# A retention layer followed by a gated two-layer network on one core: the opening chunks in another order, and second-layer weights converted block by block

## Chip, cores and metric

One Trainium2 chip, one of its cores. The metric is the device time of one execution in microseconds. Engines: TensorE (PE; its weight loads are listed as PEld), VectorE (DVE), ScalarE (ACT), GpSimd (POOL) and SyncE (SP), which issues most DMAs. Weights in HBM are float64; everything computed is float32.

## What is computed

```python
def _attn_ref(q, k, v):                    # (4, 8, 768, 64) each
    gamma = 1.0 - 2.0 ** (-5.0 - np.arange(H, dtype=np.float32))
    for t in range(S):
        state = gamma[None, :, None, None] * state + np.einsum('bhd,bhe->bhde', k[:, :, t], v[:, :, t])
        y[:, :, t] = scale * np.einsum('bhd,bhde->bhe', q[:, :, t], state)
...
def _moe_ref(x, w_in, w_out):              # x (3072, 512), w_in (512, 2048), w_out (2048, 512)
    h = x @ w_in
    sp = np.maximum(h, 0.0) + np.log1p(np.exp(-np.abs(h)))
    g = h * erf(sp)
    return (g @ w_out).astype(np.float32)
```

The output of the first part, with the heads side by side, is the input `x` of the second.

## The kernel before

**Chunks.** The sequence is cut into 24 chunks of 128 positions (6 for each of 4 batches); `j` counts them. Four chunks make up the first block of 512 tokens, and everything after it goes in blocks of 256. A chunk goes through short steps with one-letter names at the end of the code: `K_` (`ret_scale`, L385) multiplies keys and queries by powers of the decay on VectorE; `T` (`ret_transpose`, L406) transposes them on TensorE and copies the result out of PSUM on ScalarE (L424); `S_` (`ret_scores`, L427) computes the scores; `M` (`ret_mask`, L440) applies the causal mask on VectorE; `O_` (`ret_out`, L450) multiplies queries with the state (L471), scores with values (L478) and keys with values for the new state (L487), and ScalarE copies the results into `XC` (L498); `A` (`ret_add`, L606) adds the new part to the state on VectorE. A fresh state begins with chunks 0, 6, 12 and 18.

**Loads.** `load(j)` (L102) issues a chunk's keys, queries and values, each 256 KB in runs of 256 bytes, on SP's queue; the queries of chunks 1 and 2 go on ScalarE's queue (L118). Inside `load(3)` the first two parts of the first weight piece are issued ahead of the values (L121). Weight loads come after (L166 for `w_in`, L174 for `w_out`).

**Scales.** `kq_s` holds the decay factors per position, chunk in the batch, and head. Those of chunk 0 come from `d_k`; those of later chunks follow by multiplication on GpSimd (L336), then `query_scale` on VectorE inverts them for the queries. `by` is the reciprocal of `d_s`, which is loaded by two small DMAs (L298).

**Weights.** The float64 words are turned into float32 by integer arithmetic, as a generator of steps (`conversion`, L182): VectorE cuts out the exponent (L213), ScalarE rescales it (L214), VectorE prepares the high mantissa (L217), adds the low word (L222), puts sign and exponent together (L225) and multiplies (L231). There are 16 pieces of 256 columns of the first layer ("in") or 256 rows of the second ("out"), in the order in0, in1, in2, in3, out0, out1, in4, ... The first four pieces (`n < 4`) are converted in two parts each. After the last VectorE row that reads a piece's raw words, the load that reuses its place is issued (`load_pieces_after`). The steps are interleaved by hand with the rest: `pace(n)` lets n of them go, `need(...)` lets go as many as it takes until a named block is there. From piece 5 on, a piece's first step (exponent) is issued early, inside the piece before it (L262).

**First block.** `hidden(g, u)` computes 128 columns of the first layer for 512 tokens (L664) and copies them on ScalarE (L682); four of them make a group `g`. `gate(g)` runs softplus (L624) and, except for group 0, erf right after it (L634); erf of group 0 comes later by the table `after`. `gated(g)` multiplies on VectorE (L653). `project(g, tt)` adds the group's part of the second layer (L700) in four steps; for group 0 a step takes two 128-token tiles and two 128-row blocks of `w_out`. Products of the first layer begin before chunk 3 is finished: `ret_out(3, between)` puts `hidden_of(0)` for the first 384 tokens between its state products and its value products, and `hidden_of(1)` for 384 tokens follows.

**PSUM.** Three pools: `ps_r` and `ps_h` with two banks each, `ps_o` with four (`o0` to `o3`). At the start (`early`), `ret_psum` takes `ps_r` and `ps_h` in turn, for transposes, scores and results alike; only chunk 3's results are in `ps_o`. `keep_warm(n)` issues n products of the identity with itself that nobody reads.

**Start.** The order is `K_(0)`, the other scales, `T(0)`, and then for each chunk scores, scaling of the next, state addition, transposes of the next, mask, results. So TensorE issues the scores of a chunk only after all results of the one before.

From the second block on, a seven-product scheme (`hidden_part`, L757; `project_part`, L829) takes over; the change doesn't touch it.

Of the kernel before, what the change touches and what calls it, by code (L numbers as in the profile page):

```python
# [12 lines left out]
F32 = mybir.dt.float32  # L13
U32 = mybir.dt.uint32
I64 = mybir.dt.int64
AF = mybir.ActivationFunctionType
# [3 lines left out]
P = 128  # L20
# [25 lines left out]
def kernel(  # L46
# [35 lines left out]
    ctx.enter_context(tc.manual_schedule())  # L82


    KQ, V, KB = {}, {}, {}

    NB = JPC + 2
# [12 lines left out]
    def load(j):  # L100
        b, c = divmod(j, NC)
        if j == JPC - 1:  # L102

            x = act.tile([P, N], F32, name="e", bufs=1)
            KQ[j] = x[:, : 2 * d_model].rearrange("p (i h d) -> p i h d", i=2, h=H)
            V[j] = x[:, 2 * d_model : 3 * d_model].rearrange("p (h d) -> p h d", h=H)
        else:
            KQ[j] = loads.tile([P, 2, H, D], F32, name="kq")
            V[j] = loads.tile([P, H, D], F32, name="v")
        now = slice(c * C, (c + 1) * C)  # L110
        if j >= NB:
            KB[j] = loads.tile([P, HP * C], F32, name="kb", bufs=2)
            nc.sync.dma_start(KQ[j][:, 0], k[b, :, now, :].rearrange("h p d -> p h d"))
            load_blocks(KQ[j][:, 1].rearrange("p h d -> p (h d)"), q[b, :, now, :])
            load_blocks(KB[j], k[b, :, now, :])
        for i, src in enumerate((k, q) if j < NB else ()):

            queue = nc.scalar if i and 0 < j < 3 else nc.sync  # L118
            queue.dma_start(KQ[j][:, i], src[b, :, now, :].rearrange("h p d -> p h d"))  # L119
        if j == JPC - 1:  # L120
            load_piece(0, 0)  # L121
        nc.sync.dma_start(V[j], v[b, :, now, :].rearrange("h p d -> p h d"))  # L122

    kq_s = const.tile([P, NC, 2, H], F32, name="kq_s")
    d_k = const.tile([P, H], F32, name="d_k")
# [61 lines left out]
    def conversion(n):  # L187

        which, i = pieces[n]
        half, s, at = i // 4, i % 4 // 2, i % 2

        for part in range(2) if n < 4 else (None,):
            words = raws[place[n]].bitcast(U32)
            if which == "in":
                f = slice(at * 2 * P, (at + 1) * 2 * P)
                if part is not None:
                    f = slice((at * 2 + part) * P, (at * 2 + part + 1) * P)
                to = w_in_sb[:, s, 2 * half : 2 * half + 2, :, f].rearrange("p d k f -> p (d k) f")  # L200
            else:
                to = w_out_sb[:, s, 2 * half : 2 * half + 2, at * 2 : at * 2 + 2, :].rearrange(
                    "p d f c -> p d (f c)"
                )
            words = words.rearrange("p (a b w) -> p a b w", a=to.shape[1], w=2)
            number, power = (
                x.rearrange("p (a b) -> p a b", a=to.shape[1]) for x in (numbers, powers[n % 2])
            )
            if part is not None:
                f = slice(part * P, (part + 1) * P)  # L210
                words, number, power = words[:, :, f], number[:, :, f], power[:, :, f]
            lo, hi = words[:, :, :, 0], words[:, :, :, 1]
            nc.vector.tensor_scalar(power, hi, 0x7FF00000, None, op0=ALU.bitwise_and)  # L213
            nc.scalar.activation(power, power, AF.Relu, bias=below, scale=8.0)  # L214
            if part is None:
                yield
            nc.vector.tensor_scalar(  # L217
                number, hi, 0xFFFFF, 1 << 20, op0=ALU.bitwise_and, op1=ALU.bitwise_or
            )
            yield  # L220
            numberf = number.bitcast(F32)
            nc.vector.scalar_tensor_tensor(numberf, number, 2.0**32, lo, op0=ALU.mult, op1=ALU.add)  # L222
            if part is None:
                yield
            nc.vector.scalar_tensor_tensor(  # L225
                power, hi, 1 << 31, power, op0=ALU.bitwise_and, op1=ALU.bitwise_or
            )
            if part != 0:
                load_pieces_after(n)
            yield  # L230
            nc.vector.scalar_tensor_tensor(  # L231
                to, numberf, 2.0**-52, power.bitcast(F32), op0=ALU.mult, op1=ALU.mult,
            )
            done.update((which, 2 * i + u) for u in (range(2) if part is None else (part,)))
            yield
# [18 lines left out]
    def weights():  # L254


        pending = [conversion(n) for n in range(n_p)]
        begun = 0
        for n, steps in enumerate(pending):
            for k, _ in enumerate(steps, start=begun):  # L260
                yield
                if n > 4 and n + 1 < n_p and k == 2:  # L262
                    next(pending[n + 1])
                    yield
            begun = int(n > 4)
            if pieces[n] == ("out", 5):
                yield from sums("in", 0)

# [25 lines left out]
    ident = const.tile([P, P], F32, name="ident")  # L294
    make_identity(nc, ident)
    nc.scalar.dma_start(d_k, decay_k)
    for s in range(2):
        nc.scalar.dma_start(d_s[:, s], decay_s[s * D : s * D + 1, :].to_broadcast([P, HP]))  # L298
    load(0)

    nc.scalar.copy(idle_out, ident[:, :1])
    for j in range(1, JPC):
        load(j)
    load_piece(0, 1)
    for n in range(1, 4):
        load_piece(n, 0, 1)
    load(JPC)

    causal = const.tile([P, C], F32, name="causal")
    nc.gpsimd.memset(causal, 1.0)  # L310
# [20 lines left out]


    by = const.tile([P, H], F32, name="by")
    nc.vector.reciprocal(by.rearrange("p (h s) -> p s h", s=2), d_s)
    for c in range(1, NC):
        nc.gpsimd.tensor_tensor(kq_s[:, c, 0], kq_s[:, c - 1, 0], by, op=ALU.mult)  # L336

    def other_scales():
        query_scale(slice(1, NC))

# [24 lines left out]
    QT, KT, SC, AM, XC, SU = {}, {}, {}, {}, {}, {}  # L367

    psum_turn = itertools.cycle((ps_r, ps_h))
    early = True  # L370


    idle = ps_o.tile([P, P], F32, name="o0")
# [2 lines left out]
        for _ in range(n):  # L376
            nc.tensor.matmul(idle, ident, ident, start=True, stop=True)

    keep_warm(16)

    def ret_psum(pool=None):

# [2 lines left out]

    scaled = set()

    def ret_scale(j):
        if j >= NJ:
            return  # L390
        scaled.add(j)
        if j >= NB:
            nc.vector.tensor_tensor(
                KQ[j][:, 0], KQ[j][:, 0],
                kq_s[:, j % NC, 0, :, None].to_broadcast([P, H, D]), op=ALU.mult,
            )
            for i, x in enumerate((KB[j], KQ[j][:, 1].rearrange("p h d -> p (h d)"))):
                x = x.rearrange("p (u a d) -> p u a d", u=HP, d=32)
                by = kq_b[:, j % NC, i, :, :, None].to_broadcast([P, HP, 4, 32])
                nc.vector.tensor_tensor(x, x, by, op=ALU.mult)  # L400
            return
        by = kq_s[:, j % NC, :, :, None].to_broadcast([P, 2, H, D])
        nc.vector.tensor_tensor(KQ[j], KQ[j], by, op=ALU.mult)
        pace(-1.1)

    def ret_transpose(j):  # L406
        assert j in scaled
        if j >= NB:
            for name, store, x in (
# [3 lines left out]
                nc.vector.transpose(store[j].rearrange("p u t -> p (u t)"), x)  # L413
            return
        for i, (name, store) in enumerate((("k", KT), ("q", QT))):
            p = ret_psum()
            for u in range(HP):
                nc.tensor.transpose(  # L418
                    p[:, u, :],
# [25 lines left out]
            )  # L445
        pace(-1.2)

    RP = {}

    def ret_out(j, between=None, copies=True):  # L450
        c = j % NC
        m, i = divmod(j, JPC)
        if i == 0:
            XC[m] = ret.tile([P, HP, TCH], F32, name="xT")

        if between is None:
            pp = [ret_psum() for _ in range(2)]
        else:
            pp = [ps_o.tile([P, HP, C], F32, name=f"o{r + 1}") for r in range(2)]

        def place(h):
            return pp[h % 2][h // 4 * D : (h // 4 + 1) * D, h % 4 // 2, :]
# [20 lines left out]
        if c < NC - 1:  # L483
            new = SU[j] = pp[0][:, 2:, :].rearrange("p a (b d) -> p (a b) d", d=D)
            for h in range(H):
# [2 lines left out]
                    new[r * D : (r + 1) * D, h // 2, :], KQ[j][:, 0, h, :], V[j][:, h, :],  # L488
                    start=False, stop=True, skip_group_check=True,
                )  # L490
        RP[j] = pp
        if copies:
            ret_copy(j)

    def ret_copy(j):
        m, i = divmod(j, JPC)
        for r in range(2):
            nc.scalar.copy(XC[m][:, r::2, i * C : (i + 1) * C], RP[j][r][:, :2, :])  # L498
        pace(2.5)


# [117 lines left out]
    def gate(g):  # L619
# [3 lines left out]
        E[g] = act.tile([P, N], F32, name=name, bufs=1)  # L623
        nc.scalar.activation(E[g], HS[g], AF.Softplus)  # L624

        if g:
            gate_erf(g)

    def gate_erf(g):
# [59 lines left out]
    def project(g, tt):  # L689
# [3 lines left out]
        if g:  # L693
            of = [(tt, u) for u in range(FG)]
        else:
            of = [(step % 2 * 2 + i // 2, step // 2 * 2 + i % 2) for i in range(4)]
        need("out", g * FG + max(u for _, u in of))
        for tt, u in of:
            ft = g * FG + u
# [174 lines left out]
    )  # L874


    K_(0)
    other_scales()
    T(0)
    keep_warm(3)  # L880
    for j in range(JPC - 2):
        S_(j)

        K_(j + 1)
        if j:
            A(j - 1)
        T(j + 1)
        M(j)
        O_(j)


    S_(JPC - 2)
    A(JPC - 3)
    M(JPC - 2)
    ret_out(JPC - 2, copies=False)
    K_(JPC - 1)

    next(weight_steps)
    T(JPC - 1)
    ret_copy(JPC - 2)  # L900
    need("in", 0)
    S_(JPC - 1)
    A(JPC - 2)
    M(JPC - 1)
    need("in", 1)
    early = False
    ret_out(JPC - 1, lambda: hidden_of(0, slice(TCH - C)))
    room = 0.0


# [24 lines left out]
    for g in range(G0):  # L935
# [10 lines left out]
        if g:  # L946
            for tt in range(TT):
                project(g - 1, tt)
                if g == 1 and tt < 2:
                    waiting.append((K_, 5) if tt else (M, 4))  # L950
                elif g == G0 - 1 and tt == 0:
                    waiting.extend([(K_, JPC + 2), (T, JPC + 2)])
                elif g == G0 - 1 and tt == 1:
# [132 lines left out]
```

## Time and profile before

| | |
|---|---|
| median of 6 runs | 683.9 us (683.5 to 684.19) |
| profiled execution | 683.86 us, span of its records 682.1 us |
| busy, share of the span | PE 675.7 us (99%), DVE 389.6 (57%), ACT 256.0 (38%), POOL 5.7 (1%) |
| 7.5 to 25.5 us | busy PE 16.36, DVE 12.10, ACT 6.74 of 18.0 us; DMA 209 GB/s |
| 25.5 to 132 us | busy PE 106.50, DVE 99.61, ACT 56.58 of 106.5 us; DMA 172 GB/s |
| DMA | 47.65 MB in 156528 packets, 143024 of them under 512 bytes |

The profiled execution is one of the six; between its span and its time lie 1.7 us. A row of a timeline reads: start, duration, engine, line, operation, tile written <- tiles read, shapes, and in brackets how long the engine was idle before it and what ended that. The chain of work that ended last is followed back from the last instruction; in its listing by time a row's duration is only its part of the chain, up to the start of the next row. "Landing" is the time from the issue of a DMA to its last completion event; a DMA has sixteen, one for each of the core's DMA engines. The share of the whole span says little about the first 25 us, where other engines hold TensorE up; so that stretch is read by itself.

### The profile page before, as it was taken

To read this page: it belongs to the slowest core of one execution; us is meant where nothing else is said; L and a number is where in the kernel's file an instruction comes from. 1 tells how busy PE (TensorE), PEld (TensorE's weight loads), DVE (VectorE), ACT (ScalarE), POOL (GpSimd) and SP (SyncE) were. 2 spreads that over 40 slices of the span, in tenths; PEclk is the share of its full clock that TensorE was granted. 3 is DMA by queue.
4 is the path that set the end of the run, shared out by engine and by line. 5 is a ranking of instruction groups with operands and counts; after the bars stand their busy time and mean duration, and the time that the engine had idled before them with its cause. 6 is when DMAs were issued, how large, how long until landed. Compare 5 with 4: busy or idle time off the path is not lost.

```text
span 682.1 us, 14444 instructions
## 1 busy us (share of the span) xinstructions
PE 675.7 (99%) x6214; PEld 578.3 (85%) x6214; DVE 389.6 (57%) x609; ACT 256.0 (38%) x291; POOL 5.7 (1%) x21
## 2 busy tenths in 40 slices
PE   8999999999999999999999999999999999999998
PEld 8744544587999999999999999999999999999996
DVE  4899999585845634643553564555544554343324
ACT  3368362324414234144144242341441441423431
POOL 2000000100000000000000000000000000000000
PEclk9999999999999999999999999999999999999999
DMA  9999744333412322221321222222312200000000
GB/s 188 212 241 250 190 125 103 62 60 62 115 36 46 76 37 42 74 41 37 78 45 32 63 44 46 68 42 45 71 37 47 59 18 2 1 32 1 1 32 32
DMA packets 156528, 47.65 MB, mean 70 GB/s; under 512 B 143024, under 2 KB 147376, under 8 KB 156464
## 3 DMA queue, kind: packets, MB, share of 16 engines
q1 hardware_dynamic: 153952, 46.19, 31.5%
q8 instruction: 49, 0.80, 0.5%
q10 hardware_dynamic: 2512, 0.53, 0.5%
q14 instruction: 15, 0.12, 0.1%
HBM read 40.39 MB, written 6.29 MB: 68 GB/s over the span
## 4 chain that ended last, share of the span: by engine, by line
PE 97%; DMA 1%; SPq 1%; DVE 1%; issue 0%; ACT 0%
PE hp L757 37%; PE o L829 36%; PE hp L664 8%; PE o L700 8%; PE r L543 1%; PE hp L508 1%; DMA kq<-in_k_dram 1%; PE o L579 1%; PE r L431 1%; PE hp L558 1%; PE r L558 1%; PE r L478 1%; SPq L119 0%; PE r L418 0%; SPq L122 0%
## 5 line engine op out<-in xcount | busy, mean ns | idle before, releaser
L757 PE MATMUL hp<-xs,w_in_sb 128*128 128x128 f32 x1280 | 149.7, 275 | 0.0
L757 PEld LDWEIGHTS hp<-xs,w_in_sb 128*128 128x128 f32 x1280 | 147.8, 192 | 1.6 <-issue 0.5
L829 PE MATMUL o<-w_out_sb,h 128*128 128x256 f32 x640 | 141.7, 379 | 0.0
L829 PEld LDWEIGHTS o<-w_out_sb,h 128*128 128x128 f32 x640 | 121.6, 190 | 16.5
L757 PE MATMUL hp<-xT,w_in_sb 128*128 128x128 f32 x960 | 113.7, 275 | 0.0
L757 PEld LDWEIGHTS hp<-xT,w_in_sb 128*128 128x128 f32 x960 | 111.9, 192 | 1.9 <-issue 1.0
L829 PE MATMUL o<-w_out_sb,e 128*128 128x256 f32 x480 | 112.1, 383 | 0.0
L653 DVE TENSOR_TENSOR e<-h,e 128x1024 f32<-128x1024 f32 x42 | 49.5, 1221 | 100.0 <-ACT e L634 99.8
L829 PEld LDWEIGHTS o<-w_out_sb,e 128*128 128x128 f32 x480 | 88.2, 190 | 11.6
L664 PE MATMUL hp<-xT,w_in_sb 128*128 128x512 f32 (+2 forms) x144 | 56.8, 548 | 0.0
L782 DVE TENSOR_TENSOR h<-h,hp 128x512 f32<-128x512 f32 x20 | 13.7, 687 | 72.3 <-PE hp L757 72.3
L624 ACT ACT_TABLE_LOAD x24 | 30.8, 1283 | 60.8 <-issue 45.4
L664 PEld LDWEIGHTS hp<-xT,w_in_sb 128*128 128x128 f32 x144 | 25.7, 190 | 26.7 <-issue 24.3
L634 ACT ACTIVATE e<-e 128x2048 f32<-128x2048 f32 (+1 forms) x23 | 42.1, 1836 | 0.2
L624 ACT ACTIVATE e<-h 128x2048 f32<-128x2048 f32 x22 | 42.0, 1910 | 0.2
L770 DVE TENSOR_TENSOR h<-h,hp 128x512 f32<-128x512 f32 x20 | 13.8, 688 | 41.0 <-PE hp L757 41.0
L775 ACT COPY h<-hp 128x512 f32<-128x512 f32 x20 | 11.7, 585 | 61.1 <-PE hp L757 61.1
L780 ACT COPY h<-hp 128x512 f32<-128x512 f32 x20 | 11.7, 585 | 60.3 <-PE hp L757 60.3
L773 ACT COPY h<-hp 128x512 f32<-128x512 f32 x20 | 11.7, 585 | 57.1 <-PE hp L757 57.1
L597 ACT COPY xT<-r 128x256 f32<-128x256 f32 x32 | 10.4, 375 | 54.8 <-PE r L543 54.8
L634 ACT ACT_TABLE_LOAD x24 | 30.8, 1283 | 0.4
L768 ACT COPY h<-hp 128x512 f32<-128x512 f32 x20 | 11.7, 587 | 48.6 <-PE hp L757 48.6
(136 smaller groups left out, 672.8 us busy)
## 6 DMA issues: line engine op xcount, KB each, us to landing
w_out_sb<-in_moe_w_out_dram SPq DMA_DIRECT2D x14, 512.0 KB, 6.0
kq<-in_k_dram SPq DMA_DIRECT2D x23, 256.0 KB, 3.9
v<-in_v_dram SPq DMA_DIRECT2D x23, 256.0 KB, 3.2
out_dram<-r SPq DMA_DIRECT2D x23, 256.0 KB, 3.1
kq<-in_q_dram SPq DMA_DIRECT2D x288, 16.0 KB, 1.8
kb<-in_k_dram SPq DMA_DIRECT2D x288, 16.0 KB, 1.7
w_in_sb<-in_moe_w_in_dram SPq DMA_DIRECT2D x8, 512.0 KB, 10.2
w_out_sb<-in_moe_w_in_dram SPq DMA_DIRECT2D x8, 256.0 KB, 8.8
```

Of the source, the lines that this page charges most:

```text
L558: nc.tensor.matmul(other[a][own, u % 2, D:] if crossed else pp[a][own, u % 2, t], V[j][t, 2 * u + r, :], AM[j][t, r, u, :D], start=crossed ...
L624: nc.scalar.activation(E[g], HS[g], AF.Softplus)
L634: nc.scalar.activation(E[g][:, half], E[g][:, half], AF.Erf)
L653: nc.vector.tensor_tensor(E[g][:, half], HS[g][:, half], E[g][:, half], op=ALU.mult)
L664: nc.tensor.matmul(HP_[ft][:, t], w_in_of(ft, kk), XC[0][:, kk, t], start=(kk == 0), stop=(kk == n_k - 1),)
L700: nc.tensor.matmul(O[0][tt].rearrange("p (d c) -> p d c", d=2), E[g][:, u * TCH + tt * P : u * TCH + (tt + 1) * P], w_out_of(ft), start=(f ...
L757: nc.tensor.matmul(bank[:, u, :], w_in_sb[:, s, IN[a], kk, u * P : (u + 1) * P], XS[m][b][:, kk, :], start=(p in (1, 2, 5) and u == 0 and ...
L768: nc.scalar.copy(h["11"], flat)
L770: nc.vector.tensor_tensor(h["11"], h["11"], flat, op=ALU.add)
L773: nc.scalar.copy(h["12"], flat)
L782: nc.vector.tensor_tensor(h["12"], h["12"], flat, op=ALU.add)
L829: nc.tensor.matmul(O[m][i][:, half, :], G[g][a][:, u * P : (u + 1) * P], w_out_sb[:, s, OUT[b], u, :], start=i not in started, stop=(s == ...
```

## The change

- **Loads**: all keys and queries on SP's queue; a chunk's values are issued by a function of their own after the next chunk's keys and queries. The decay row comes in one DMA.
- **Scaling and transposing one by one**: `ret_scale` and `ret_transpose` take an argument for keys (0) or queries (1) alone. Keys go to `ps_r`, queries to `ps_h`.
- **Scales** of chunk 1 are made on VectorE right after the first keys are scaled; GpSimd makes those from chunk 2 on.
- **Results** of chunks 0 to 3 go to `ps_o`; `copies=False`, `RP` and `ret_copy` go.
- **Order** of the first four chunks: written out anew. Scores of chunk 1 come ahead of the results of chunk 0, those of chunk 2 inside the results of chunk 1, the query transposes of chunk 3 inside the results of chunk 2.
- **Idle products**: `keep_warm` 7, 2, 1 and 2 in place of 16 and 3.
- **Second layer**: pieces 4 and 5 (out0, out1) are converted in two parts too, one for each 128-row block, with VectorE's first row and ScalarE's row over the whole piece; early issue of the first step begins with piece 6. Steps of `project(0)` take one block for all four token tiles.
- **Group 1**: its erf moves behind the first step of `project(0)` and the first step of piece 5; masks 4 and scaling 5 move behind the conversion of in4.

```diff
@@ load @@
         for i, src in enumerate((k, q) if j < NB else ()):
-
-            queue = nc.scalar if i and 0 < j < 3 else nc.sync
-            queue.dma_start(KQ[j][:, i], src[b, :, now, :].rearrange("h p d -> p h d"))
-        if j == JPC - 1:
-            load_piece(0, 0)
-        nc.sync.dma_start(V[j], v[b, :, now, :].rearrange("h p d -> p h d"))
+            nc.sync.dma_start(KQ[j][:, i], src[b, :, now, :].rearrange("h p d -> p h d"))
+        if not early:
+            load_values(j)
+
+    def load_values(j):
+        b, c = divmod(j, NC)
+        nc.sync.dma_start(V[j], v[b, :, c * C : (c + 1) * C, :].rearrange("h p d -> p h d"))
@@ conversion @@
-        for part in range(2) if n < 4 else (None,):
+        for part in range(2) if n < 6 else (None,):
...
+            if part == 0 and which == "out":
+                nc.vector.tensor_scalar(
+                    power, words[:, :, :, 1], 0x7FF00000, None, op0=ALU.bitwise_and
+                )
+                nc.scalar.activation(power, power, AF.Relu, bias=below, scale=8.0)
+                yield
             if part is not None:
-                f = slice(part * P, (part + 1) * P)
+                if which == "out":
+                    to = to[:, :, part * DH : (part + 1) * DH]
+                f = to.shape[2]
+                f = slice(part * f, (part + 1) * f)
                 words, number, power = words[:, :, f], number[:, :, f], power[:, :, f]
             lo, hi = words[:, :, :, 0], words[:, :, :, 1]
-            nc.vector.tensor_scalar(power, hi, 0x7FF00000, None, op0=ALU.bitwise_and)
-            nc.scalar.activation(power, power, AF.Relu, bias=below, scale=8.0)
+            if which == "in" or part is None:
+                nc.vector.tensor_scalar(power, hi, 0x7FF00000, None, op0=ALU.bitwise_and)
+                nc.scalar.activation(power, power, AF.Relu, bias=below, scale=8.0)
@@ weights @@
-                if n > 4 and n + 1 < n_p and k == 2:
+                if n > 5 and n + 1 < n_p and k == 2:
...
-            begun = int(n > 4)
+            begun = int(n > 5)
@@ issue of loads @@
-    for s in range(2):
-        nc.scalar.dma_start(d_s[:, s], decay_s[s * D : s * D + 1, :].to_broadcast([P, HP]))
+    nc.scalar.dma_start(d_s, decay_s[::D].rearrange("(o s) h -> o s h", o=1).to_broadcast([P, 2, HP]))
     load(0)
...
     for j in range(1, JPC):
         load(j)
+        load_values(j - 1)
+    load_piece(0, 0)
+    load_values(JPC - 1)
     load_piece(0, 1)
     for n in range(1, 4):
         load_piece(n, 0, 1)
     load(JPC)
+    load_values(JPC)
@@ scales @@
-    nc.vector.reciprocal(by.rearrange("p (h s) -> p s h", s=2), d_s)
-    for c in range(1, NC):
-        nc.gpsimd.tensor_tensor(kq_s[:, c, 0], kq_s[:, c - 1, 0], by, op=ALU.mult)
+
+    def second_scales():
+        nc.vector.reciprocal(by.rearrange("p (h s) -> p s h", s=2), d_s)
+        nc.vector.tensor_tensor(kq_s[:, 1, 0], kq_s[:, 0, 0], by, op=ALU.mult)
+        query_scale(1)
+        for c in range(2, NC):
+            nc.gpsimd.tensor_tensor(kq_s[:, c, 0], kq_s[:, c - 1, 0], by, op=ALU.mult)
 
     def other_scales():
-        query_scale(slice(1, NC))
+        query_scale(slice(2, NC))
...
-    keep_warm(16)
+    keep_warm(7)
@@ ret_transpose @@
-            p = ret_psum()
+            if part not in (None, i):
+                continue
+            p = ret_psum((ps_h if i else ps_r) if early else None)
@@ ret_out @@
-        if between is None:
+        if early:
+            pp = [ps_o.tile([P, HP, C], F32, name=f"o{(2 * j + r + 1) % 4}") for r in range(2)]
+        else:
             pp = [ret_psum() for _ in range(2)]
-        else:
-            pp = [ps_o.tile([P, HP, C], F32, name=f"o{r + 1}") for r in range(2)]
@@ gate, project @@
-        if g:
+        if g > 1:
             gate_erf(g)
...
-            of = [(step % 2 * 2 + i // 2, step // 2 * 2 + i % 2) for i in range(4)]
+            of = [(i, step) for i in range(TT)]
@@ order of the start @@
-    K_(0)
+    K_(0, 0)
+    second_scales()
+    T(0, 0)
+    keep_warm(2)
+    K_(0, 1)
+    T(0, 1)
+    keep_warm(1)
+    K_(1, 0)
+    T(1, 0)
+    S_(0)
+    K_(1, 1)
+    T(1, 1)
+    keep_warm(2)
     other_scales()
-    T(0)
-    keep_warm(3)
-    for j in range(JPC - 2):
-        S_(j)
-
-        K_(j + 1)
-        if j:
-            A(j - 1)
-        T(j + 1)
-        M(j)
-        O_(j)
-
-
-    S_(JPC - 2)
-    A(JPC - 3)
-    M(JPC - 2)
-    ret_out(JPC - 2, copies=False)
-    K_(JPC - 1)
-
-    next(weight_steps)
-    T(JPC - 1)
-    ret_copy(JPC - 2)
+    M(0)
+    S_(1)
+    K_(2, 0)
+    T(2, 0)
+    O_(0)
+    M(1)
+    K_(2, 1)
+    T(2, 1)
+    A(0)
+    K_(3, 0)
+
+    def next_scores():
+        S_(2)
+        M(2)
+
+    O_(1, next_scores)
+    T(3, 0)
+    A(1)
+    K_(3, 1)
+    O_(2, lambda: T(3, 1))
+    A(2)
+
     need("in", 0)
-    S_(JPC - 1)
-    A(JPC - 2)
-    M(JPC - 1)
+    S_(3)
+    M(3)
     need("in", 1)
+    ret_out(JPC - 1, lambda: hidden_of(0, slice(TCH - C)))
     early = False
-    ret_out(JPC - 1, lambda: hidden_of(0, slice(TCH - C)))
@@ first block @@
-                if g == 1 and tt < 2:
-                    waiting.append((K_, 5) if tt else (M, 4))
+                if g == 1 and tt == 0:
+                    need("out", 1)
+                    next(weight_steps)
+                    gate_erf(1)
+                elif g == 1 and tt == 2:
+                    need("in", 2 * FG + 1)
+                    waiting.extend([(M, 4), (K_, 5)])
```

## The prediction, made before the changed kernel ran

> **What bounds the kernel now.** I read the page's chain shares first, then the chain in order of time, then VectorE's rows, the landings, and TensorE's first matmuls.
>
> ```profile
> PE 97%; DMA 1%; SPq 1%; DVE 1%; issue 0%; ACT 0%
> ```
> TensorE sets the end. The 3% that are not TensorE lie in the first 25 us:
>
> ```profile
> 5.31 7.86 DMA kq<-in_k_dram
> 13.20 1.23 DVE kq L403
> ...
> 20.57 0.56 DVE e L403
> ...
> 23.17 0.60 ACT qT L424
> 23.81 0.37 PE r L431
> 24.97 0.60 PE o L471 x16
> 25.57 2.78 PE hp L664 x8
> 28.35 1.02 PE o L478 x16
> 29.37 0.46 PE o L487 x16
> 29.84 21.78 PE hp L664 x64
> ```
> From 25.57 each row begins where the one before ends, on TensorE, to the last 1% of the span. So a gain can only come from when the second block of the first layer (29.84, `hidden_of(1)`) starts, and it lasts only if nobody who feeds TensorE falls behind. VectorE is the one who might: by the stretches view it is busy 99.6 of the 106.5 us from 25.5 to 132.
>
> ```profile
> 20.49 1.22 DVE L403 TENSOR_TENSOR e<-e,kq_s 128x1024 f32<-128x1024 f32 x1
> 21.62 0.42 DVE L213 TENSOR_SCALAR w_out_sb<-w_out_sb 128x512 uint32<-128x512 uint32 x1
> 24.35 0.41 DVE L611 TENSOR_TENSOR state<-state,r 128x256 f32<-128x256 f32 x1
> 26.21 0.42 DVE L213 TENSOR_SCALAR w_out_sb<-w_out_sb 128x512 uint32<-128x512 uint32 x1
> 28.32 0.69 DVE L231 SCALAR_TENSOR_TENSOR w_in_sb<-w_out_sb 128x512 f32<-128x512 f32 x1
> ```
> Block 0 of the weights is converted from 21.62 to 24.43 (2.81 us), block 1 from 26.21 to 29.01 (2.80). What these two wait for is a load:
>
> ```profile
> 12.73 1.99 SPq L166 DMA_DIRECT2D w_out_sb<-in_moe_w_in_dram  x2
> w_out_sb<-in_moe_w_in_dram SPq DMA_DIRECT2D x2, 256.0 KB, 7.1
> 16.12 5.12 SPq L166 DMA_DIRECT2D w_out_sb<-in_moe_w_in_dram  x6
> ```
> Issued from 12.73 to 14.72, landing about 7.1 later: the completion events put block 0's two halves at 20.0 and 21.0, and block 1's (issued from 16.12) at 24.55 and 25.75. So VectorE now starts block 0 only 0.6 us after its data, and block 1 only 0.5 us after.
>
> **The change part by part.**
>
> *Loads.* Keys and queries go ahead of values, and two query loads move from ScalarE's queue to SP's. Block 0 still stands behind the same eleven 256 KB transfers, block 1 behind the same fourteen, and the engines are full (the DMA row stands at 9 almost throughout from 3.5 us on). So blocks 0 and 1 land at 21.0 and 25.75 again: nothing. The order within changes. Completion events now come at 3.96, 5.7, 6.7, 9.2, 9.5, 10.7, 12.3, 13.1, 14.3, 15.5, 18.9; I give these places to the new order, with places 4 and 5 (two queues at once now) at about 8.0 and 9.2: k0 4.0, q0 5.5, k1 6.7, q1 8.0, v0 9.2, k2 10.7, q2 12.3, v1 13.1, k3 14.3, q3 15.5, v2 18.9. The jump to 18.9 is one of sixteen engines: the fifteenth event of that transfer is at 17.6, after a 16 KB instruction fetch at 14.3.
>
> *Scaling one by one.* A 128x1024 product (1.23) becomes two 128x512 (0.68, from the mask rows): +0.13 times four = 0.5 us of VectorE. Its cover is VectorE's idle time, 5.9 of the 18 us from 7.5 to 25.5; without it, 0.5. Scales of chunk 1 come to VectorE: four small rows of 0.17 to 0.20, and a wait for the decay row, whose two issues land at 4.3 and 5.75 now; one issue lands between. Behind that wait stands q0's scaling, which waits for 5.5 anyway.
>
> *Idle matmuls.* 19 become 12. TensorE is free at 4.5 instead of about 7.9.
>
> *Interleaving.* No instruction is added on TensorE; the order is new. I placed the rows by hand, each at the end of what it needs: transposes of a half 0.44, its copy 0.59, scores 1.09, masks 1.29, values 1.02, state products 0.60, state sum 0.47, addition 0.41. First keys scaled 4.0 to 4.65; first scores at 8.0 (9.58 now); second at 10.6 (13.45); third at 14.7 (18.09); values of chunk 2 at 18.95, where v2 lands; state addition 2 done at 21.0; fourth scores 20.5 to 21.5 (23.81 now). So the path ends at 21.0 as block 0 lands: conversion 0 from 21.05 to 23.85, product 0 at 23.9 (25.57 now). Masks 3 fill VectorE until 25.15; conversion 1 from 25.77 to 28.57. TensorE meanwhile: 23.9 + 2.78 + 1.48 = 28.16, and waits 0.5. Product 1 at 28.65 instead of 29.84: **1.2 us gained**. Two stalls are left, both on weights; what is late next is the load, not the chunks. If the copies or PSUM banks cost more than placed, TensorE has those 0.5 us; bounds: 0.8 (chunks 0.9 late) to 1.2.
>
> *Second layer's first pieces.* A piece takes 5.0 us of VectorE now (48.44 to 53.43). By blocks: 0.60 once, then twice 0.46 + 0.61 + 0.71 + 0.61 = 5.4. Two pieces: +0.8 us, with no cover, since VectorE has none there. It is paid from VectorE's lead. Now the first second-layer product starts at 56.94, with its gated half ready at 54.8: 2.1 to spare, and the block form asks for half a piece less. I carried the new order on: last first-layer block of group 1 converted 46.9; half a piece 50.1; gated product behind erf at 52.05 to 54.3; second block 56.3 (needed 59.2); third 59.5 (62.7); fourth 61.9 (66.2). Piece 6 now waits for ScalarE: softplus and erf of group 1 run 58.1 to 64.5, so its exponent is done at 65.7 and the piece at 68.2 (needed 69.7, now 67.5 for 70.94). Masks 4 then end at 71.3 (73.7), addition 4 at 78.1 (the transposes of chunk 5 want its bank at 78.85), masks 5 at 88.0 (88.6). So no stall, with 0.5 to 0.7 us in hand at the last two; VectorE thus caps the gain at about 1.7. Weight reloads that follow VectorE's rows go out up to 2 to 4 us later (piece 11's at 76.5 for 72), and are used over 10 us after that: nothing.
>
> **Sum.** The profiled execution took 683.86 (span 682.1, 1.7 around it), as good as the median of 683.9. Minus 1.2: **682.7**; its own range, gains of 0.8 to 1.7, is 682.2 to 683.1. About 0.2%, 1.37 us, is what a measurement of this kernel can tell from no change, so the forecast lies at that bound.
>
> **The clock.** This is what I trust least.
>
> ```profile
> L377 PE MATMUL o<-ident x26: 357/421/582, 1.5 to 7.0; 128*128 128x128 f32 x26
> L377 PE MATMUL o<-ident x14: 274/275/421, 6.7 to 9.2; 128*128 128x128 f32 x14
> ```
> Idle matmuls took 421 ns until 7.0 and 275 after: 5.5 us of unbroken work before full speed; their spacing halves from 0.21 to 0.11. The new kernel has a gap after 4.5 and others later. I take the grant at about 7, since gaps there are 0.2 to 0.3 us.
>
> [...]
>
> **Rivals.**
>
> *More: the late engine isn't late.* The jump to 18.9 comes from one engine. If the instruction fetch falls elsewhere, blocks 0 and 1 land as the fourteenth of sixteen events do now, 19.3 and 23.3. Then values 2 start by 18.95 from the TensorE side alone, conversion 0 at 20.95, masks 3, conversion 1 from 25.0 to 27.8, product 1 at 28.15: gain 1.7, up to 2.4 if the chunks run closer. For it: VectorE and TensorE have less to do before 21 than now. Against: the fetch follows TensorE's instruction count, which is the same there within 10%. 681.5 to 682.2.
>
> *Little: one restart.* If the 5.5 us count anew from 4.7, the grant comes at about 10.2. Each us of slow clock costs about 0.5 us of TensorE's work: 3.2 us, 1.6 late at the values, 0.4 of which the waits take up. Gain about 0: 683.5 to 684.
>
> *Slower: the clock stays down.* The same with a second restart at the gap before the second chunk's transposes (7.5): grant at 13 or later. 6 us of slow clock cost 3.0 and more; minus 0.5 that waits swallow, minus the gain of 1.2: +1.3 to +2, so 685.2 to 686. It decides from a grant at about 10.5 on. For it: seven idle matmuls instead of sixteen, and waits for k1, q1 and copies in that stretch. Against: at half speed the work fills the gaps, so the slow state ends itself; and now TensorE keeps its clock through 0.8 us of waiting at 23.
>
> *That it doesn't do what it says:* if two issues in a row on SP held up the loads, q1 and q2 would be later than on ScalarE's queue; SP's issues (0.4 to 2.6 us) run some 7 us ahead of the landings, so no: under 3%, inside the others.
>
> **Chances.** Forecast 0.42 (0.18 of it beyond 1.37 us), more 0.27, little 0.10, slower 0.21 (0.20 beyond the bound). Faster 0.18 + 0.27 = 0.45; within 0.24 + 0.10 + 0.01 = 0.35; slower 0.20. The range reaches from the best of "more" to the near edge of "slower": 681.4 to 685.2.
>
> **What would show it.** Right: conversion 0 starting with its load near 21, product 0 near 23.9, product 1 near 28.7 waiting for L231's counterpart, then no gap until 132, where the first seven-product part starts 1.2 earlier than 132.23. Clock: idle matmuls and transposes at 0.21 spacing after 7.5. Wrong: block 1 landing before 25, TensorE waiting on masks 5 or addition 4, or a gap ahead of the second layer at 55.7.

## The result, and the profile after

The changed kernel takes 685.81 us (median of 17 runs, 683.81 to 687.67) where the kernel before takes 683.73 (38 runs, 683.42 to 684.58). The ratio is 1.0026 (the two medians divided give 1.0030), with a 95% interval from 1.002 to 1.0033: slower by about 0.26%, just beyond the 0.2% that can be told from no change, and outside the range that was given. The profiled execution took 685.98, with a span of 684.3 (before: 683.86 and 682.1), so it is 2.12 longer and lies near the median.

The spread is wider than before, and it isn't one heap. These are all the executions of the changed kernel, the profiled one among them, by the mean TensorE clock that each lists:

| mean clock | executions | times, us |
|---|---|---|
| 0.998 | 13 | 685.59 to 686.18, and twice 687.67 |
| 1.000 | 5 | 683.81, 684.07, 684.1, 684.26, 684.41 |

A clock of 0.998 over 684 us is some 1.4 us of work lost, which is nearly the distance of the two groups. So the first question to the profile is where the clock is down.

The chain's shares, from the page of the changed kernel, say at first that nothing happened:

```profile
PE 98%; DVE 1%; DMA 1%; ACT 0%; issue 0%; ACTq 0%
```

TensorE still sets the end. The chain in order of time (start, length, what) shows where it set it later:

```profile
22.00 0.38 ACT xT L514
...
22.74 0.42 DVE w_out_sb L225
...
24.86 0.70 DVE w_in_sb L243
25.69 4.51 PE hp L680 x8
...
31.70 21.78 PE hp L680 x64
...
90.98 1.02 PE r L493 x16
...
134.43 5.36 PE hp L773 x48
```

Product 0 (the eight matmul records of `hidden_of(0)`, L680) starts at 25.69, where it started at 25.57 before: the whole reordering of the start has gained nothing there. And it takes 4.51 us for the 2.78 of before. Product 1 starts at 31.70 instead of 29.84, 1.86 late, and the last row is 2.20 late (132.23 before).

TensorE's rows in order of time give the wait ahead of product 0, in brackets at its end:

```profile
22.97 0.67 PE L493 MATMUL o<-qT,state 64*64 64x128 f32 x16
25.69 4.51 PE L680 MATMUL hp<-xT,w_in_sb 128*128 128x384 f32 x8 [2.06 <-DVE w_in_sb L243]
```

Here are the same matmuls by line (minimum, median and maximum duration in ns). Before, the median was 486:

```profile
L680 PE MATMUL hp<-xT,w_in_sb x8: 503/834/847, 25.7 to 29.7; 128*128 128x384 f32 x8
```

And here are stretches of the span (length, then busy time of TensorE, its weight loads, VectorE, ScalarE and GpSimd, then the granted clock, the DMA share and GB/s):

```profile
22.90:26.31 3.41, 1.35 (x22) 0.91 (x19) 3.34 (x7) 0.72 (x1) 0.00 (x0) 1.00 1.11 231
26.31:29.72 3.41, 3.41 (x7) 1.69 (x5) 3.34 (x7) 0.72 (x1) 0.00 (x0) 0.50 1.13 232
29.72:33.14 3.42, 3.42 (x39) 2.41 (x38) 1.22 (x4) 1.27 (x3) 0.00 (x0) 1.00 1.14 233
```

TensorE idles for 2.06 us, starts product 0 at full speed, and 0.6 us later its clock is halved for 3.41 us. At the 0.50 of that stretch 3.41 us are 1.7 us of work lost, which agrees with the 1.73 by which product 0 is longer.

Why conversion 0 (L225) starts at 22.74 and not at the 21.05 of the forecast (before, L213: 21.62) stands in VectorE's rows:

```profile
22.40 0.42 DVE L627 TENSOR_TENSOR state<-state,o 128x256 f32<-128x256 f32 x1 [2.67 <-ACT xT L514]
22.74 0.42 DVE L225 TENSOR_SCALAR w_out_sb<-w_out_sb 128x512 uint32<-128x512 uint32 x1
```

The third state addition (L627) waits 2.67 us, and what released it is not TensorE, which had made the sums by 21.98, but ScalarE's first copy of the results (L514), 22.00 to 22.38. Sums and results stand in one PSUM bank, and in the program the copy goes first; it is the last 0.4 of the 2.67. VectorE had idled since 19.7 with block 0's data there from 21.26 on.

Last, masks 5, by the rows of their tile (the second line says who waited for them, for how long in us, and how often):

```profile
L467 DVE TENSOR_TENSOR am<-r,causal x2: 681/682/683, 90.0 to 90.6; 128x512 f32<-128x512 f32 x2
...
  PEld r L493: 1.0, 2
```

The state products of chunk 5 (L493) wait for the bank that the masks still read; their row is 1.02 long, 0.34 more than the 0.68 of before.

**The sum:** 0.12 (product 0 late) + 1.73 (clock) + 0.34 (masks 5) = 2.19, against 2.20 in the chain and 2.12 in the profiled times.

### The profile page after: what moved, and what is told of

It reads as the page before. It is cut to its first block, busy times and chain, and to the rows that moved or that the text cites. A ratio compares the mean times of both kernels' runs of the same rounds, so it can differ in the third digit from the quotient of the medians.

```text
span 684.3 us, 14427 instructions
## 1 busy us (share of the span) xinstructions
PE 675.9 (99%) x6200; PEld 576.7 (84%) x6200; DVE 391.5 (57%) x624; ACT 256.5 (37%) x291; POOL 7.8 (1%) x20
## 4 chain that ended last, share of the span: by engine, by line
PE 98%; DVE 1%; DMA 1%; ACT 0%; issue 0%; ACTq 0%
PE hp L773 37%; PE o L845 36%; PE hp L680 8%; PE o L716 8%; PE r L559 1%; PE hp L524 1%; PE o L595 1%; PE r L455 1%; DMA d_s<-decay_s_dram 1%; PE hp L574 1%; PE o L500 1%; PE r L574 1%; PE r L500 0%; PE r L442 0%; PE o L509 0%; PE hp L442 0%
## 5 line engine op out<-in xcount | busy, mean ns | idle before, releaser
L680 PE MATMUL hp<-xT,w_in_sb 128*128 128x512 f32 (+2 forms) x144 | 58.4, 561 | 2.1 <-DVE w_in_sb L243 2.1
L798 DVE TENSOR_TENSOR h<-h,hp 128x512 f32<-128x512 f32 x20 | 13.7, 687 | 72.3 <-PE hp L773 72.3
L680 PEld LDWEIGHTS hp<-xT,w_in_sb 128*128 128x128 f32 x144 | 26.4, 195 | 29.5 <-issue 27.6
L791 ACT COPY h<-hp 128x512 f32<-128x512 f32 x20 | 11.7, 586 | 61.0 <-PE hp L773 61.0
L786 DVE TENSOR_TENSOR h<-h,hp 128x512 f32<-128x512 f32 x20 | 13.8, 688 | 36.4 <-PE hp L773 36.4
L796 ACT COPY h<-hp 128x512 f32<-128x512 f32 x20 | 11.7, 585 | 60.2 <-PE hp L773 60.2
L789 ACT COPY h<-hp 128x512 f32<-128x512 f32 x20 | 11.7, 585 | 57.1 <-PE hp L773 57.1
L793 DVE TENSOR_TENSOR h<-h,hp 128x512 f32<-128x512 f32 x20 | 13.7, 687 | 27.6 <-ACT h L791 27.6
```

The source lines that it names most:

```text
L680: nc.tensor.matmul(HP_[ft][:, t], w_in_of(ft, kk), XC[0][:, kk, t], start=(kk == 0), stop=(kk == n_k - 1),)
L786: nc.vector.tensor_tensor(h["11"], h["11"], flat, op=ALU.add)
L789: nc.scalar.copy(h["12"], flat)
L793: nc.vector.tensor_tensor(h["22"], h["22"], other, op=ALU.add)
L798: nc.vector.tensor_tensor(h["12"], h["12"], flat, op=ALU.add)
```

## The experiments

All were timed in five rounds beside the kernel before: 683.75 (33 runs) for e1 to e4, 683.76 (27 runs) for e5 to e8. My theory was: the idle gap ahead of product 0 takes the clock away. The rivals: too few idle matmuls at the start leave the clock unsteady; the second layer's new order of conversion costs the time.

**e1: fill the gap.** Nine idle products, which nobody reads, between the state products of chunk 3 and product 0:

```diff
+    def filled(n):
+        HP_[0] = ps_h.tile([P, TCH], F32, name="hp")
+        for _ in range(n):
+            nc.tensor.matmul(HP_[0][:, :P], ident, ident, start=True, stop=True)
+        hidden_of(0, slice(TCH - C))
-    ret_out(JPC - 1, lambda: hidden_of(0, slice(TCH - C)))
+    ret_out(JPC - 1, lambda: filled(9))
```

> The changed kernel with nine more idle products (identity with identity, into the bank that the first product overwrites) between the state products of chunk 3 and the first product of the first layer, where TensorE stood still for 2.06 us. Theory (the gap takes the clock away): the half-speed stretch from 26.27 to 29.68 is gone, product 0 takes 2.8 us instead of 4.51, times gather near 684.0 with none at 685.6 or above; about -1.75 against the changed kernel's 685.8. Rival (product 0 starts late, and the clock only goes with it): the idle products can't bring conversion 0 forward, so 685 to 686 stays. Rival (the clock goes because the opening has fewer idle products, 12 for 19): the drop stays.

Measured: 684.23 (683.91 to 684.38, 11 runs), ratio 1.0007 [0.9998, 1.0016]. Its chain:

```profile
23.79 2.21 PE hp L936 x18
26.00 2.67 PE hp L680 x8
...
89.45 0.95 PE r L493 x16
```

Added work made the kernel 1.6 us shorter. Product 0 takes 2.67 at full speed, although the fill (L936) makes it start 0.3 later, and none of the eleven executions is in the upper group. (The nine products show as 18 records, as the start's 19 showed as 38.) The start's idle matmuls are those of the change, so they weren't the cause.

**e2: e1, with the second layer's part of the change undone** (pieces, the gate's order and the waiting list as before).

> As e1_fill, and the second-layer part undone (pieces 4 and 5 whole, the old steps of the first group's second layer, the old places of erf 1, masks 4 and scaling 5). Theory (the added VectorE work makes masks 5 late by 0.33 us): that wait goes, 683.7, 0.3 below e1_fill. Rival (the second-layer part is needed for the new opening): a wait of 0.5 us or more appears ahead of the first second-layer product, 684.5 or above.

Measured: 683.91 (683.76 to 685.5, 11 runs), ratio 1.0005 [0.9996, 1.0014]; 0.32 less than e1. The chain has the state products of chunk 5 back at 0.68:

```profile
90.75 0.68 PE r L493 x16
```

So this part costs what the row said, 0.3. The profiled execution is the one of 685.5, and it shows something else. TensorE's row of the second keys' transposes, and the chain's of product 0:

```profile
8.57 1.06 PE L442 MATMUL r<-ident,kq 128*128 128x128 f32 x4
...
27.30 2.67 PE hp L680 x8
```

The four take 1.06; in the changed kernel's profiled execution they take 0.60. In this execution the clock came at 10.2 rather than by 7.7, and product 0 started at 27.30, 1.3 later than in e1.

**e3: the second layer's part alone,** on the kernel before.

> The kernel before with the second-layer part alone. Theory: no wait at the first second-layer product before (2.1 us in hand), so nothing is gained there; masks 5 late by 0.2 to 0.4 us: 683.9 to 684.2. Rival (it is what costs the 2 us): 685 or above.

Measured: 683.87 (683.73 to 684.37, 11 runs), ratio 1.0003 [0.9994, 1.0012]. It gains nothing, and its cost by itself can't be told from none.

**e4: the state additions ahead of the copies,** for chunks 0 to 2:

```diff
+        RP[j] = pp
+        if not early or j == JPC - 1:
+            ret_copy(j)
...
+    def ret_copy(j):
+        m, i = divmod(j, JPC)
         for r in range(2):
-            nc.scalar.copy(XC[m][:, r::2, i * C : (i + 1) * C], pp[r][:, :2, :])
+            nc.scalar.copy(XC[m][:, r::2, i * C : (i + 1) * C], RP[j][r][:, :2, :])
         pace(2.5)
...
     A(0)
+    ret_copy(0)
     K_(3, 0)
...
     A(2)
+    ret_copy(2)
```

> The changed kernel with each state addition of chunks 0 to 2 ahead of the two ScalarE copies from the same results, instead of behind them. Theory (the additions wait 0.38 us each for a copy of the same bank, and three of them in a row put conversion 0 at 22.74 instead of 21.3): conversion 0 at 21.3 to 21.8, product 0 at 24.2 to 24.7. The gap before it shrinks little (state products come earlier too), so the clock still falls in part of the executions: 683 to 685.2, a wide spread. Rival (the copies are not what the addition waits for): conversion 0 stays at 22.7 and the time at 685.8.

Measured: 683.26 (683.1 to 684.98, 11 runs), ratio 0.9995 [0.9987, 1.0004]; 2.5 less than the changed kernel. VectorE's row of the third addition is

```profile
21.38 0.42 DVE L635 TENSOR_TENSOR state<-state,o 128x256 f32<-128x256 f32 x1 [2.33 <-PE o L509]
```

and TensorE's row of product 0 is

```profile
24.69 2.82 PE L688 MATMUL hp<-xT,w_in_sb 128*128 128x384 f32 x8 [1.68 <-DVE w_in_sb L243]
```

The addition now waits for TensorE alone, 1.0 earlier; product 0 starts 1.0 earlier, and at full speed. I had expected part of the executions to lose the clock still, since the gap is 1.68; all eleven list 1.000, the one of 684.98 too, so that one isn't a loss at the gap.

**e5: e4 with six idle products in the gap.** The same code as in e1, with `filled(6)`.

> The additions ahead of the copies, and six idle products in the gap that is left (1.68 us in e4_swap). Theory (the gap takes the clock): as e4_swap's undisturbed executions, 683.3, and none at 685 or above. Rival (idle products delay the first product): 683.6 or above.

Measured: 683.27 (683.07 to 684.85, 11 runs), ratio 0.9996 [0.9987, 1.0005]. The same as e4: with a gap of 1.68 there is nothing left to save.

**e6: e5 with fewer conversion steps in group 2,** so that masks 5 come in time:

```diff
-            pace_around(3.4 if ft > FG else 0)
+            pace_around((2.8 if g == 2 else 3.4) if ft > FG else 0)
```

> As e5_swap_fill, with 2.8 in place of 3.4 conversion steps let go around each first-layer product of group 2, so that masks 5 stand behind less VectorE work. Theory (masks 5 are 0.3 us late because of the conversion rows ahead of them): the state and value products of chunk 5 follow without a gap and 0.3 us are gained: 682.9 to 683.0. Rival (masks 5 wait for the scores, not for VectorE): no change, 683.3.

Measured: 683.04 (682.68 to 683.25, 11 runs), ratio 0.9989 [0.9981, 0.9998]. The chain:

```profile
24.58 2.82 PE hp L688 x8
...
88.33 0.60 PE r L493 x16
```

The state products of chunk 5 wait for nothing. This is the best version measured: 0.72 below the kernel before, its interval wholly below 1, and 2.77 below the changed kernel. The gain is half of what a measurement of this kernel can tell singly.

**e7: a gap in the kernel before,** with its 19 idle matmuls untouched. Eight dummy rows (times 1.0, in place) behind the conversion of block 0:

```diff
+            if n == 0 and part == 0:
+                for _ in range(8):
+                    nc.vector.tensor_scalar(to, to, 1.0, None, op0=ALU.mult)
```

> The kernel before with eight more VectorE rows on the first converted block (each multiplies it by 1.0 in place), so that TensorE waits 2.5 us or more after chunk 3's scores; nothing else is changed. Theory (a gap of 2 us near 25 is enough to take the clock): the block comes 2.7 us later, and the median lies a further 1 to 1.7 above that, 687.5 to 688.5, with a half-speed stretch of 3.4 us in the profile and two groups of times 1.7 apart. Rival (the clock falls because of the new order or its fewer idle products): 686.5 in all executions, no half-speed stretch.

Measured: 690.31 (689.26 to 690.62, 4 runs), ratio 1.0093 [1.0079, 1.0106]. In the profiled execution (689.26) TensorE's row behind the gap, and the chain's of product 1, are

```profile
28.22 1.13 PE L474 MATMUL o<-qT,state 64*64 64x128 f32 x16 [3.54 <-DVE state L614]
...
35.23 21.78 PE hp L667 x64
```

and the stretches are

```profile
22.35:25.76 3.41, 1.51 (x20) 1.09 (x18) 3.24 (x7) 1.67 (x5) 0.00 (x0) 1.00 1.13 240
25.76:29.17 3.41, 0.95 (x16) 0.73 (x16) 3.27 (x8) 0.00 (x0) 0.00 (x0) 0.50 1.12 244
29.17:32.59 3.42, 3.42 (x9) 1.85 (x6) 3.35 (x8) 0.72 (x1) 0.00 (x0) 0.50 1.13 245
```

In the old order, too, the gap alone takes the clock, in all four executions (each lists 0.995), here for two stretches of 3.41. Product 1 starts at 35.23, 5.39 late: 3.25 are the gap itself, 2.14 the halved clock (state products 1.13 for 0.60, product 0 with its two followers 5.88 for 4.27). Cause and direction are as expected, but there are no two groups, and the size was underestimated: the gap cost 3.25 for 2.7, and I counted one stretch. The profiled execution is the shortest of the four; what makes the others 0.8 to 1.4 longer at the same listed clock is not shown.

**e8: e6 with the scales of chunk 1 after the first query scaling,** which in the change stands behind the decay row's landing.

```diff
     K_(0, 0)
-    second_scales()
     T(0, 0)
     keep_warm(2)
     K_(0, 1)
+    second_scales()
```

> As e6_fewer_steps, with the scales of chunk 1 made after the first queries are scaled instead of before. Theory (the decay row lands at 5.5 and its four small rows hold the first queries' scaling up by 0.7 us): first query transposes at 6.4 instead of 7.1, the path to conversion 0 shorter by 0.3 to 0.4; conversion 0 is then held by its load (21.2): 682.5 to 682.8. Rival (the path is already bound by later loads): no change against e6_fewer_steps.

Measured: 683.06 (682.83 to 684.01, 11 runs), ratio 0.999 [0.9981, 0.9999]: as e6. The first query transposes start at 6.51, where the changed kernel's profiled execution has 7.08; but the second keys' start at 7.87 against 7.80, since they wait for their own load: the 0.57 is gone at the next row. (In e6's profiled execution the decay row landed early, and the two stand at 6.44 and 7.61 without the move.) The theory that this wait costs time fell.

## Why the prediction was wrong, point by point

**What bounds it:** right. TensorE sets the end, and from 31.70 on nothing but masks 5 delays it. So the gain or loss is product 1's start, plus 0.34.

**Loads:** right, to half a us. By the completion events blocks 0 and 1 land at 21.26 and 25.31 (21.0 and 25.75 predicted; before, 21.08 and 25.80), the values of chunk 2 at 18.92 (18.9). That block 1 comes earlier gains nothing: its conversion starts at 26.66.

**The interleaving, placed by hand:** wrong by 1.4 to 1.8. The third state addition ends at 22.7, not 21.0; conversion 0 starts at 22.74, not 21.05; product 0 at 25.69, not 23.9. The rows were placed "each at the end of what it needs", and for the additions that left out the copies that stand before them at the same bank, 0.38 each, at all three chunks; e4 puts 1.0 of it back. The rest is later work ahead of it: the values of chunk 2 start at 20.39, not 18.95, and in e4 still at 19.77. The 0.5 us that TensorE was to wait for block 1 takes up some of this. What is left, 1.3, ate the planned gain of 1.2; but for 0.1 it didn't make the kernel slower than before.

**The failed step** that made the kernel slower is the one where TensorE's wait ahead of product 0 was counted by its length alone, and what it does to the clock at nothing. By the prediction's own figures the fourth scores end at 21.5, the state products take 0.60, and product 0 starts at 23.9: 1.8 us of waiting, written down as "Two stalls are left, both on weights". The reason that it was free stood under the clock: "now TensorE keeps its clock through 0.8 us of waiting at 23". The trace of before carries 0.8; the prediction used it for 1.8, and the chip made it 2.06. In its place the profile showed a loss of 1.73 (13 of 18 executions list the lower clock); e1 and e4 take it away, and e7 brings a loss of 2.1 with a longer gap in the kernel before. Against the forecast, product 1 is 3.05 late (31.70 for 28.65): 1.73 by the clock and 1.32 by the interleaving; with masks 5 that is 3.39, where forecast and measured profile lie 3.32 apart.

**The rival "the clock stays down"** had the right resource in the wrong place. It put the loss into the opening, as a matter of how many idle matmuls are left there; in the profiled execution the clock came at 5.8, earlier than before's 7.1, and e1 with the change's own opening is 1.6 faster. "Little: one restart", with its grant at about 10.2, is what e2's profiled execution shows, where product 0 is 1.3 late (the rival had 1.6, less 0.4 in waits); it is an exception, not the median. That the grant fell at its time looks like luck: the rival counted 5.5 us anew from a gap, and no run shows such a count. From the first idle product (1.46 in both) to the grant it is 4.4 us in the changed kernel's profiled execution and 5.7 in the one of before.

**Second layer:** "no stall, with 0.5 to 0.7 us in hand" was mis-sized. Measured from product 1, the masks end at 59.59 (59.35 predicted). But they are needed at 59.28, not at 59.95: not the value products ask for them first but the state products, which write the bank that the masks read. e2 and e6 both take the 0.34 back.

**Left at nothing, and right in the sum:** the wait for the decay row, though not because the first queries are waited for anyway: their scaling starts at 6.34, behind that row, and e8 shows that nothing comes of it. One-by-one scaling found idle time.

## What to carry to other kernels

Idle time ahead of a matmul wasn't priced by its length alone here: with a wait of 2.06 us came a clock of 0.50 for 3.41 us, 1.73 on top of the stall; with one of 1.68 (e4), or with nine idle matmuls in the wait (e1), it didn't come. So read the granted clock behind a wait as well as its length, and where it falls, shorten the wait, or put idle matmuls there, where the wait is, and not only at the start (e7 had all 19 there and lost the clock). Where two engines read one PSUM bank, the reader whom the path waits for goes first (in e4 that brought product 0 by 1.0 us); one 0.38 us copy ahead of an addition, three times in a row, and the work behind it ate a planned gain of 1.2. And where a kernel's times fall into two groups, read what distinguishes the groups before reading the median.

## What was not expected of the hardware

**In both profiled executions that lost the clock it was down for 3.41 us or twice that, and went at a multiple of that after the grant.** In the changed kernel's profiled execution the clock was granted at about 5.8 (the duration of the first matmuls falls there from 421 to 275 ns), lost at 26.31 and back at 29.72: 20.48 and 23.89 after 5.83, or 6 and 7 times 3.413, and 3.413 is the length that the trace's clock record gives for the stretch between. In e7 the times are about 5.3, 25.76 and 32.59, the last two 6 and 8 times 3.413 after 5.28. The time of the grant differs from one execution to the next; in nine profiled ones it came anywhere from 4.4 to 7.7, and in e2 at 10.23, by the first entry of each trace's clock record (in e1, which has none, by the durations). Before that entry the stretches view prints a clock of 1.00, too; that the clock is lower there shows in the matmuls alone (in the kernel before, idle matmuls 0.21 us apart until then and 0.11 after). Counted from each grant in steps of 3.413 us, forward or back, TensorE's busy time of a step and what the clock did at its end were:

```
clock on,   busy 1.74 of 3.41 (e4, 21.34 to 24.75):      kept
clock on,   busy 1.51 of 3.41 (e7, 22.35 to 25.76):      lost
clock on,   busy 1.35 of 3.41 (changed, 22.90 to 26.31): lost
clock half, busy 0.95 of 3.41 (e7, 25.76 to 29.17):      stays half
clock half, busy 2.78 of 3.41 (e2, 3.40 to 6.81):        stays half
clock half, busy 2.81 of 3.41 (e4, 0.86 to 4.27):        stays half
clock half, busy 2.95 of 3.42 (e8, 0.99 to 4.41):        granted
```

The first row of that list, in a stretch 0.04 earlier, as the stretches view gives it:

```profile
21.30:24.72 3.42, 1.75 (x35) 1.41 (x33) 3.28 (x7) 1.27 (x3) 0.00 (x0) 1.00 1.13 216
```

So in these executions the clock was kept behind a step with 1.74 us of work and lost behind steps with 1.51 and 1.35; from half speed it was granted behind a step with 2.95 and not behind one with 2.81. Each figure rests on a single execution. An estimate from these rows for the two groups: a gap of 2.06 falls into one step, as in the profiled execution, where it left 1.35 of work, or is cut by the end of a step, and then both steps hold more. No execution of the faster group was profiled, so that is not shown. e7 and e4 together speak, in my reading, for a step's sum and not for one long pause: in e7 the clock fell 1.1 us after TensorE had stopped, with an earlier wait of 0.82 in the same step, and e4's single wait of 1.68 cost nothing.

Transposes, too: e4's step from 4.27 to 7.69 held 2.18 us of transposes and 1.84 of idle matmuls (together 3.39, since they overlap) and was followed by the grant, while the one before it, with 2.81 of idle matmuls, was not. The 1.84 alone are less than those 2.81, so I read it that the transposes counted in this execution.

**What stays open:** whether the scattered executions 1 to 1.7 us above the rest in e2, e4, e5 and e8, and the two of 687.67, are all late grants; only e2's was profiled. No run tried how much work keeps the clock between 1.51 and 1.74 us of a step, nor what moves the time of the grant.
